# First batch's v sums taken from float32 operands, a weight decode without maximum and mask, eleven-column statistics and a new instruction order, in an attention and gated-MLP kernel on one core

## The chip, the cores and the metric

The kernel runs on one core of a Trainium2 chip. The metric is device time in microseconds (us). Engines are named as the profile names them: PE (matrix products; PEld is its weight load), DVE (vector), ACT (activation), POOL (general) and SP, which here only issues DMAs.

## The reference

Sliding-window attention, whose output is the input of a gated MLP with a spatial gate:

```
scores = q k^T / 8 + slope_h * -|i-j|, masked to 0 <= i-j < 128     # 8 batches, 8 heads, 576 x 64
attn   = softmax(scores);  x = attn v, heads side by side            # x: 8 x 576 x 512
h      = gelu_tanh(x @ w_in);  u, v = halves of h                    # w_in: 512 x 1024
v_n    = (v - mean v) / sqrt(var v + 1e-6) * g_ln                    # along the 512 features
v_s    = w_sg @ v_n + b_sg                                           # along the 576 positions
out    = x + (u * v_s) @ w_out
```

All inputs are float32.

## The kernel before

The kernel works through 32 pairs of heads (four a batch) and, for each batch, through an MLP. Its schedule is one hand-searched list, `ORDER`, in which every step has a short name; the list is the program order on each engine, since each instruction is tied to the one before it on its engine. An instruction that waits therefore holds all that stands behind it on its engine.

Steps of pair n: `q` and `L` load; `a`, `c` are the scores (`*` both at once, from pair 5 on), line 247; `A` `B` `C` `G` add the bias and take minima on DVE (lines 273, 266); `e` `E` `f` `F` `j` exponentials on ACT (line 282); `R` adds 1e-9 to the sums and inverts them on DVE (lines 294, 295); `r` `s` `S` scale on POOL (line 299); `t` `T` `z` transpose on PE (lines 309, 322); `X` `Y` copy the transposes out with masks on DVE (line 318); `2`/`3` and `v`/`V` multiply with the values on PE (lines 329, 342); `x` gathers the result in float32 (`xf`), `h` and `l` split it into a high and a low part in fp32r (`xs`, lines 356, 359).

A product of float32 numbers in the MLP is made of three fp32r products, high x high, high x low and low x high, by `mm3` (lines 559 to 561). Weights arrive as int64 views of float64 and are decoded (`split64`): `i` loads, `d` scales the low word and takes the absolute value of the high word on ACT (lines 179, 181), `m` (line 183) takes a maximum on DVE, `b` (185) shifts and masks, `o` (187) puts the sign and top exponent bits back, `+` (190, POOL) adds the low word, `H` (192, ACT) writes the high part, `-` (194, DVE or POOL by turns) the low part. Twelve tiles are decoded: `w_in` as 0 to 7 (0 to 3 hold the half for v) and `w_out` as 8 to 11. The decoded float32 tile of `w_in` is kept in `scratch` (named `tmp` in the trace), whose memory later becomes `vn`.

Steps of the MLP of batch b: `v` and, in batch 0, `w` sum x times the v half; each of the four row blocks t is the sum of four 128-row pieces c, so batch 0 has 16 such steps, `w{t}{c}` and `v0{t}` for the last c. `tt` sums the last 64 rows. `vg`, `tg` are the gelu (line 633, 658); `n..b/p/c/h` and `vn`/`tn` the normalisation (lines 579 to 595). `u{b}{f}{i}` sums the u half, `uc` copies and `ug` is its gelu; `y{b}{f}{i}` is the spatial product (lines 559 to 561, 706, 707), `gm` `gh` `gl` gate it and split it (lines 712, 716, 719), `O`/`Oa` is the output product, `oa` adds x (line 742), `D` stores (line 754).

So `u000` is the first u product of batch 0 and `y000` its first spatial product. A pool of two PSUM buffers, `ps_m`, serves all MLP sums in the order of their allocation.

Of the kernel before, what the change touches and what calls it, by code (L numbers as in the profile page):

```python
# [21 lines left out]
def attention_gmlp(  # L22
# [148 lines left out]
    def split64(hi, lo, w, f, last):  # L171


        w0 = w.bitcast(U32).rearrange("p (n t) -> p n t", t=2)[:, :, 0]
# [6 lines left out]
        nc.scalar.activation(f, w1f, AF.Abs)
        yield
        nc.vector.tensor_scalar(f, f, TINY64, None, ALU.max)
# [8 lines left out]
        nc.scalar.activation(hi, f, AF.Copy)  # L192
        yield
        last.tensor_tensor(lo, f, hi.bitcast(F32), ALU.subtract)
        yield
# [581 lines left out]
    for b in range(B):  # L777
# [7 lines left out]
        T2 l1 q5 d6 G3 z2 +4 Y2 a4 F3 L3 P2 j3 -2 A4 22 v2 k1 H4 m6 e4 R3 -4 B4 i3 w21 x2 o5 c4 b6 h2 L5 r3 w11 j4 s3 C4
        w31 E4 G4 S3 t3 f4 w01 X3 F4 l2 i10 T3 d3 z3 Y3 +5 w12 q6 P3 k2 R4 *5 o6 H5 m3 i11 -5 b3 w22 A5 s4 q7 w32 +6 e5
        B5 23 w02 v3 j5 o3 i8 C5 S4 E5 H6 G5 +3 L4 x3 f5 r4 t4 -6 h3 T4 X4 d11 l3 i9 z4 Y4 H3 d8 -3 m11 k3 v03 P4 m8 F5
        b11 24 v01 b8 R5 v4 o11 vg03 o8 vg01 s5 nv30b v02 x4 r5 v00 nv30c nv10b nv30p t5 z5 S5 d9 X5 +11 nv30h T5 P5 +8
        d10 Y5 nv10p H11 35 m10 H8 V5 vn03 -11 vg00 nv10c u000 nv00b -8 L6 x5 nv10h b10 *6 vn01 nv00c vg02 L7 o10 u001 A6
        +10 nv20b u010 nv00p uc00 B6 q8 nv20p nv00h nv20c H10 u011 vn00 nv20h bl m9 C6 -10 tt0 uc01 G6 vn02 u020 bH b9  # L790
        tj0 u021 o9 tg0 b- u030 nt0b +9 uc02 nt0c H9 u031 nt0p -9 nt0h *7 uc03 tn0 ug0 y000 q9 A7 B7 h5 y020 h4 l5 C7 G7
        y001 l4 j6 k5 F6 y021 k4 E6 gm00 f6 e6 y010 gm02 E7 R6 s6 j7 y011 gh00 S6 f7 gh02 gl00 y030 gm01 e7 gh01 r6 gl02
        F7 z6 t6 y031 P6 X6 gl01 R7 T6 s7 gm03 Oa0 Y6 gh03 S7 gl03 *8 r7 O02 q10 A8 e8 B8 E8 C8 O00 j8 G8 f8 36 z7 oa00
        t7 V6 P7 oa02 F8 D00 D02 R8 s8 T7 L9 x6 X7 O03 S8 h6 Y7 l6 r8 37 k6 oa03 V7 D03 O01 L8 x7 h7 l7 *9 oa01 k7 D01
# [10 lines left out]
        S14 oa10 v23 Y13 r14 D10 vg22 nv22b t14 vg23 nv22c u230 x12 nv22p nv32b nv22h 313 nv32c V13 vn22 nv32p u231 L15
        x13 X14 nv32h *15 uc23 vn23 ug2 L14 y210 A15 h13 B15 h12 z14 l13 y220 q17 P14 C15 l12 G15 k13 T14 y211 Y14 e15
        E15 *16 gm21 F15 f15 y200 gh21 q19 A16 j15 gl21 B16 e16 y221 E16 C16 R15 f16 G16 y201 s15 gm22 F16 S15 gh22 t15
        gm20 j16 y230 gl22 gh20 R16 k12 gl20 314 y231 r16 s16 V14 gm23 S16 gh23 r15 Oa2 gl23 x14 X15 h14 l14 T15 O23 Y15
        k14 z15 t16 oa23 P15 O20 D23 315 T16 oa20 V15 D20 O21 L16 x15 X16 h15 Y16 l15 L17 *17 oa21 k15 u300 A17 q18 e17
# [5 lines left out]
        z19 y331 gm31 P19 gh31 gl31 V17 gm33 gh33 Oa3 gl33 L18 x17 X19 h17 l17 T19 O32 Y19 k17 z18 t18 oa32 P18 319 O30
        D32 V19 oa30 D30 T18 L20 x19 X18 O33 h19 Y18 l19 k19 318 oa33 V18 D33 O31 L21 x18 h18 l18 *20 oa31 k18 D31 u400
        A20 e20 B20 tt4 j20 C20 f20 G20 u401 tj4 E20 F20 *21 uc40 R20 s20 u430 q22 A21 r20 tg4 S20 B21 t20 q23 v40 C21
        e21 nt4b E21 j21 nt4c u431 f21 G21 nt4p nt4h X20 T20 v41 F21 tn4 uc43 Y20 R21 v42 vg40 r21 s21 vg41 nv04b S21
        nv14b nv04p v43 nv14c nv04c nv14p nv04h nv14h vn40 z20 u420 vn41 vg42 P20 vg43 nv24b *22 nv34b nv24p nv34c u410
# [58 lines left out]
```

## Time and profile before

| | us |
|---|---|
| median of 3 runs | 641.43 |
| lowest, highest run | 639.53, 645.07 |
| the profiled execution's span, first to last instruction | 639.6 |
| PE busy in it | 606.7 |
| DVE, ACT, POOL busy in it | 385.3, 356.2, 236.7 |

In these slices of a fortieth of the span a digit is the busy share in tenths:

```profile
PE   4877789999999999999999999999999999999997
DVE  5899788445854587545753577547664465452611
```

The span is the profiled execution's own time, 1.8 us under the median of the runs. Times in the views count from the span's start. A group's row reads: line, engine, operation, written tile<-read tiles, shapes, xcount | busy us, mean ns of one | idle time before it and what ended it.

### The profile page before, as it was taken

The numbers are of one execution on the slowest core, as the hardware profiler recorded it, in microseconds if no ns is written. First come the engines' busy times: TensorE is split into PE (matmuls) and PEld (weight loads), VectorE is DVE, ScalarE is ACT, GpSimd is POOL, SyncE is SP. The second block draws the span as 40 slices with busy tenths as digits, with TensorE's granted clock in tenths as the row PEclk, the third lists the DMA queues.
The fourth block names the chain that finished last, engine by engine and source line by source line (L and its number), as shares of the span: only waits on it lengthen the run. The fifth ranks groups of instructions, "written<-read, shape, count | busy, mean of one in ns | idle before, by whom it ended". The sixth has DMA issues, their size and how long they took to land.

```text
span 639.6 us, 14817 instructions
## 1 busy us (share of the span) xinstructions
PE 606.7 (95%) x5664; PEld 552.6 (86%) x5664; DVE 385.3 (60%) x1297; ACT 356.2 (56%) x1045; POOL 236.7 (37%) x237
## 2 busy tenths in 40 slices
PE   4877789999999999999999999999999999999997
...
DVE  5899788445854587545753577547664465452611
...
GB/s 277 261 214 180 107 116 38 1 172 57 40 114 70 141 38 104 71 78 98 93 38 58 173 38 76 79 95 115 40 93 73 103 94 40 40 39 38 0 1 75
DMA packets 55931, 57.24 MB, mean 89 GB/s; under 512 B 8498, under 2 KB 45362, under 8 KB 55860
## 3 DMA queue, kind: packets, MB, share of 16 engines
...
## 4 chain that ended last, share of the span: by engine, by line
PE 84%; DVE 8%; ACT 2%; issue 2%; POOL 1%; DMA 1%; SPq 0%; POOLq 0%; DVEq 0%
PE ps_m L559 20%; PE ps_m L561 19%; PE ps_m L560 19%; PE ps_s L342 7%; PE ps_s L247 4%; PE ps_a L309 4%; PE ps_a L247 3%; DVE e L266 2%; DVE px L318 2%; PE ps_a L342 1%; PE ps_m L707 1%; PE ps_m L706 1%; DVE tmp L187 1%; PE ps_m L643 1%; PE ps_m L645 1%
## 5 line engine op out<-in xcount | busy, mean ns | idle before, releaser
L282 ACT ACTIVATE e<-e,stats 128x128 f32<-128x128 f32 (+1 forms) x320 | 121.1, 380 | 33.8 <-DVE stats L266 32.5
L299 POOL TENSOR_TENSOR e<-e,rr 128x512 f32<-128x512 f32 (+1 forms) x96 | 79.9, 853 | 130.4 <-DVE rr L295 103.0
L559 PE MATMUL ps_m<-ws,vn 128*128 128x288 f32 x256 | 79.1, 309 | 0.0
L559 PE MATMUL ps_m<-g,wo 128*128 128x288 f32 x256 | 78.8, 308 | 0.0
L559 PE MATMUL ps_m<-xs,wi 128*128 128x288 f32 x256 | 78.4, 306 | 0.1
L561 PE MATMUL ps_m<-g,wo 128*128 128x288 f32 x256 | 75.9, 296 | 0.0
L561 PE MATMUL ps_m<-xs,wi 128*128 128x288 f32 x256 | 75.7, 296 | 0.0
L561 PE MATMUL ps_m<-ws,vn 128*128 128x288 f32 x256 | 75.7, 296 | 0.0
L560 PE MATMUL ps_m<-xs,wi 128*128 128x288 f32 x256 | 75.6, 295 | 0.0
L560 PE MATMUL ps_m<-ws,vn 128*128 128x288 f32 x256 | 75.6, 295 | 0.0
L560 PE MATMUL ps_m<-g,wo 128*128 128x288 f32 x256 | 75.0, 293 | 0.5 <-POOL g L719 0.5
L359 POOL TENSOR_TENSOR xs<-xf,xs 128x576 fp32r<-128x576 f32 x32 | 45.8, 1432 | 77.8 <-ACT xs L356 77.6
L318 DVE TENSOR_TENSOR px<-ps_a,m_old 128x512 f32<-128x512 f32 x64 | 43.9, 687 | 49.5 <-PE ps_a L309 37.0
L584 POOL TENSOR_TENSOR rs<-rs,mhalf 128x1 f32<-128x1 f32 (+1 forms) x40 | 32.6, 814 | 96.7 <-DVE rs L581 90.1
L719 POOL TENSOR_TENSOR g<-u,g 128x576 fp32r<-128x576 f32 x32 | 45.5, 1423 | 52.3 <-ACT g L716 52.2
L282 ACT ACTIVATION_READ_ACCUMULATOR e<-e,stats 128x1 f32 (+1 forms) x320 | 60.1, 188 | 0.0
L742 DVE TENSOR_TENSOR xf<-ps_m,xf 128x576 f32<-128x576 f32 x32 | 24.1, 757 | 58.4 <-PE ps_m L561 58.4
L712 DVE TENSOR_TENSOR u<-ps_m,u 128x576 f32<-128x576 f32 x32 | 24.2, 755 | 51.2 <-PE ps_m L707 51.2
L559 PE MATMUL ps_m<-wi,xs 128*128 128x512 f32 x128 | 53.7, 419 | 0.5 <-ACT wi L192 0.5
L247 PE MATMUL ps_s<-qk 64*64 64x192 f32 (+2 forms) x632 | 42.5, 351 | 11.3 <-DMA qk<-qkT 7.3
L559 PEld LDWEIGHTS ps_m<-xs,wi 128*128 128x128 f32 x256 | 48.3, 189 | 4.1 <-issue 1.9
L561 PE MATMUL ps_m<-wi,xs 128*128 128x512 f32 x128 | 51.2, 400 | 0.7 <-POOL xs L359 0.7
...
## 6 DMA issues: line engine op xcount, KB each, us to landing
...
outT<-xf SPq DMA_DIRECT2D x32, 288.0 KB, 2.1
...
wst<-w_sgT SPq DMA_DIRECT2D x4, 288.0 KB, 5.9
vd<-v_in SPq DMA_DIRECT2D x64, 16.0 KB, 2.6
```

What stands on the lines that cost most here:

```text
L247: return lambda: nc.tensor.matmul(dst, qk[js, 0, q0:q0 + R], qk[js, 1, k0:k1], start=True, stop=True)
L282: nc.scalar.activation(x, x, AF.Exp, bias=self.nm[0:n, i:i + 1], scale=-1.0, accum_out=self.sm[0:n, i:i + 1])
L299: nc.gpsimd.tensor_tensor(x, x, self.rr[0:n, i:i + m].rearrange("p (m o) -> p m o", o=1).broadcast_to([n, m, c]), ALU.mult)
L309: burst([lambda t=t: nc.tensor.transpose(ct[:, t * P:(t + 1) * P], self.pr[j][:, t, :], ident) for t in range(T)])
L318: nc.vector.tensor_tensor(xv[:, :, :, i, :], cv, m.rearrange("p (t h c) -> p t h c", t=1, h=1).broadcast_to([P, T, 2, R]), ALU.mult)
L342: return lambda: nc.tensor.matmul(x1[heads[j], q0 + lo // 2 * R if t < 0 else q0 + t * R:q0 + (hi + 1) // 2 * R], block, px[j][:, (half * ...
L359: nc.gpsimd.tensor_tensor(lo_of(self.xs), self.xf, hi_of(self.xs).bitcast(F32), ALU.subtract)
L559: nc.tensor.matmul(dst, ah, bh, start=(first and i == 0), stop=False)
L560: nc.tensor.matmul(dst, ah, bl, start=False, stop=False)
L561: nc.tensor.matmul(dst, al, bh, start=False, stop=(last and i == n - 1))
L584: nc.gpsimd.tensor_tensor(x["rs"][0:rows], x["rs"][0:rows], mhalf[0:rows], ALU.pow)
L719: nc.gpsimd.tensor_tensor(st[f"g{f}"][:, 1, :], st["u"][:, f, :], st[f"g{f}"][:, 0, :].bitcast(F32), ALU.subtract)
```

## The change

1. `m` is gone: the absolute value is taken with a scale that makes the rebased exponent come out by a plain shift, `b` shifts without a mask, and `o` takes only the sign from the source. The twelve DVE instructions of line 183 go.
2. In batch 0 each of the 16 steps `w`/`v0` is one float32 product, of `xf` and `scratch`, in place of the three fp32r products of `mm3`. They wait for `x` and `+` in place of `h`, `l`, `H` and `-`.
3. The statistics tiles and `rr` have eleven columns for each half in place of ten; the eleventh holds ones.
4. The normalised `vn` of batch 0 may be written once all eight `-` steps are done (before: 7 and 3), since `scratch` is read by the products now.
5. `ORDER` is another list, without the `m` steps. It differs nearly everywhere.

```diff
-    TINY64 = 2.0 ** -15
+    REBASE = 2.0 ** (-(1023 - 127) // 8)
...
-        x = const.tile([P, 2, NS], F32, name=f"stats{i}")
+        x = const.tile([P, 2, NS + 1], F32, name=f"stats{i}")
...
-        nc.scalar.activation(f, w1f, AF.Abs)
+        nc.scalar.activation(f, w1f, AF.Abs, scale=REBASE)
         yield
-        nc.vector.tensor_scalar(f, f, TINY64, None, ALU.max)
+        nc.vector.tensor_scalar(fi, fi, 3, None, ALU.logical_shift_left)
         yield
-        nc.vector.tensor_scalar(fi, fi, 3, 0x3FFFFFFF, ALU.logical_shift_left, ALU.bitwise_and)
-        yield
-        nc.vector.scalar_tensor_tensor(out=fi, in0=w1, scalar=-0x40000000, in1=fi, op0=ALU.bitwise_and, op1=ALU.bitwise_or)
+        nc.vector.scalar_tensor_tensor(out=fi, in0=w1, scalar=-0x80000000, in1=fi, op0=ALU.bitwise_and, op1=ALU.bitwise_or)
...
-            rr = self.rr = att.tile([P, NS], F32, name="rr", bufs=3)
+            rr = self.rr = att.tile([P, NS + 1], F32, name="rr", bufs=3)
...
-        add(f"m{k}", "DVE", 0.34, at, go, [f"d{k}"], port=True)
-        add(f"b{k}", "DVE", 0.43, at, go, [f"m{k}"], port=True)
+        add(f"b{k}", "DVE", 0.43, at, go, [f"d{k}"], port=True)
...
-        add(k + "h", "ACT", 1.25 if key == "t" else 0.63, at, high, [k + "p", k + "c", f"y{b - 1}{NF - 1}1" if b else "-7", f"y{b - 1}{NF - 1}0" if b else "-3"])
+        add(k + "h", "ACT", 1.25 if key == "t" else 0.63, at, high, [k + "p", k + "c"] + ([f"y{b - 1}{NF - 1}{i}" for i in range(2)] if b else [f"-{c}" for c in range(2 * NC)]))
...
                 for c in cs:
+                    if b == 0:
+                        nc.tensor.matmul(st[key][:, t % 2, :], x[c][:, ts], scratch[:, c, :], start=(c == 0), stop=(c == NC - 1))
+                        continue
...
-                        add(f"w{t}{c}" if c < NC - 1 else f"v{b}{t}", "PE", 0.75, pair_at(c) + OPEN, v_sum(t, [c]), [f"h{c}", f"l{c}", f"-{c}", f"H{c}", f"w{t}{c - 1}" if c else None, f"w{t2}0" if i else None], take=take if c == 0 and i == 0 else [])
+                        add(f"w{t}{c}" if c < NC - 1 else f"v{b}{t}", "PE", 0.75, pair_at(c) + OPEN, v_sum(t, [c]), [f"x{c}", f"+{c}", f"w{t}{c - 1}" if c else None, f"w{t2}0" if i else None], take=take if c == 0 and i == 0 else [])
...
-        i0 q0 i7 d0 wl2 m0 a0 b0 i1 o0 A0 d7 +0 q1 B0 wH2 H0 m7 c0 L1 w-2 d1 C0 -0 G0 e0 b7 wl0 a1 m1 j0 o7 q2 b1 E0 A1
+        q0 a0 wl0 i0 i7 q1 i4 wH0 A0 B0 w-0 d7 d0 d4 b7 b0 o0 +0 E0 e0 j0 c0 C0 G0 f0 F0 b4 o7 R0 L0 a1 A1 B1 i1 d1 i2 e1 s0
...
-        O73 oa72 D72 O71 oa73 D73 oa71 D71
+        O72 oa72 O71 oa71 D63 D62 D72 D70 D60 D73 D61 D71
```

From the first removed line on, the new program's line numbers differ by a few: `R` is on 292 and 293, the new `v` sums on 625, `mm3` on 556 to 558.

DVE in the opening, right after the second block of minima of pair 0 (`C0`, `G0`; rows of line 266 or 264 are its additions and minima). Before:

```order
L273 COPY_PREDICATED ps_s<-sel,ps_s 128x2x64
L266 ISA e,stats_135<-ps_s,bias_108 128x128
L266 ISA stats_135 128x1
L266 ISA e,stats_135<-ps_s,bias_108 128x128
L266 ISA stats_135 128x1
L185 TENSOR_SCALAR tmp<-tmp 128x512
L183 TENSOR_SCALAR tmp<-tmp 128x512
L187 SCALAR_TENSOR_TENSOR tmp<-wst,tmp 128x512
L185 TENSOR_SCALAR tmp<-tmp 128x512
```

Now:

```order
L271 COPY_PREDICATED ps_s<-sel,ps_s 128x2x64
L264 ISA e,stats_135<-ps_s,bias_108 128x128
L264 ISA stats_135 128x1
L264 ISA e,stats_135<-ps_s,bias_108 128x128
L264 ISA stats_135 128x1
L183 TENSOR_SCALAR tmp<-tmp 128x512
L185 SCALAR_TENSOR_TENSOR tmp<-wst,tmp 128x512
L292 TENSOR_SCALAR rr<-stats_135 128x11
L293 RECIPROCAL rr<-rr 128x11
```

Each decode has two DVE instructions now (183 is the shift, 185 the sign) and `R0` follows the decode of tile 4 at once; before, the first blocks of pair 1 stood ahead of `R0`.

PE at the first v sum, after the second part of the scores of pair 2 (line 247, now 245). Before:

```order
L247 MATMUL ps_s<-qk 64x192 x8
L309 MATMUL ps_a<-ident,e 128x128 x8
L559 MATMUL ps_m<-wi,xs 128x512
L560 MATMUL ps_m<-wi,xs 128x512
L561 MATMUL ps_m<-wi,xs 128x512
L322 MATMUL ps_a<-ident,e_1_133 128x128
```

Now:

```order
L245 MATMUL ps_s<-qk 64x192 x8
L307 MATMUL ps_a<-ident,e 128x128 x4
L625 MATMUL ps_m<-tmp,xf 128x512
L307 MATMUL ps_a<-ident,e 128x128 x4
L625 MATMUL ps_m<-tmp,xf 128x512
L320 MATMUL ps_a<-ident,e_1_133 128x128
```

One product stands where three stood, and two row blocks are summed between the transposes of pair 1.

PE just ahead of `u000`, the first product of `xs` with 288 columns. Before:

```order
L309 MATMUL ps_a<-ident,e 128x128 x4
L322 MATMUL ps_a<-ident,e_1_133 128x128
L309 MATMUL ps_a<-ident,e 128x128 x4
L329 MATMUL ps_s<-p_2_130,vd_128 128x64
L342 MATMUL ps_s<-px,vt 64x64 x2
L342 MATMUL ps_s<-px,vt 64x128 x12
L342 MATMUL ps_s<-px,vt 64x64 x4
L559 MATMUL ps_m<-xs,wi 128x288
```

Now:

```order
L340 MATMUL ps_a<-px,vt 64x64 x2
L340 MATMUL ps_a<-px,vt 64x128 x12
L340 MATMUL ps_a<-px,vt 64x64 x4
L625 MATMUL ps_m<-tmp,xf 128x512 x2
L307 MATMUL ps_a<-ident,e 128x128 x4
L556 MATMUL ps_m<-xs,wi 128x288
```

Before, all of pair 5 (`t5 z5 T5 35 V5`) stood ahead of `u000`; now only `t5` does, and `z5`, `T5`, `35`, `V5` come among the u products.

More of the change, by code (lines that the diff above doesn't have):

```diff
@@ L785, in attention_gmlp @@
[L785 to L794, printed above, removed]
@@ L805, in attention_gmlp @@
[L805 to L809, printed above, removed]
@@ L815, in attention_gmlp @@
[L815 to L819, printed above, removed]
@@ L835, in attention_gmlp @@
-        328 t29 vn61 nv06h V28 vn60 tj6 u621 x28 X29 tg6 u630 uc62 nt6b u610 nt6c nt6p u631 nt6h tn6 u611 uc63 T29 uc61
-        y600 Y29 h28 ug6 l28 *31 k28 y620 A31 B31 y601 C31 e31 f31 G31 y621 gm60 F31 gh60 y630 j31 gm62 gl60 E31 gh62 329
-        R31 V29 gl62 s31 y610 L31 x29 r31 S31 h29 z31 t31 l29 P31 y611 X31 L30 k29 y631 gm61 gh61 *30 gl61 gm63 gh63 Oa6
-        gl63 A30 e30 B30 T31 j30 C30 O61 Y31 f30 E30 G30 F30 331 V31 R30 oa61 s30 D61 S30 t30 x31 O60 X30 r30 h31 z30 P30
-        oa60 l31 T30 Y30 D60 O63 k31 330 oa63 V30 D63 O62 x30 h30 l30 oa62 u700 k30 D62 tt7 u701 tj7 uc70 u720 tg7 u721
@@ new lines, in attention_gmlp @@
+        w11 23 B5 R4 v3 C5 -6 e5 E5 j5 f5 G5 -5 x3 w02 tl i11 i10 wl1 L4 gb L5 s4 r4 S4 h3 k0 F5 t4 X4 v03 T4 vg03 l2 l3 -2
+        w12 z4 v01 Y4 P4 H3 24 w22 v4 nv30b -3 R5 nv30c nv30p vg01 wH1 d11 v00 nv30h x4 v02 nv10b s5 vn03 nv10c b11 vg00
+        nv10p k3 k1 nv10h o11 vn01 vg02 +11 t5 u000 u001 u010 nv00b nv20b nv00p uc00 d10 nv00c b10 X5 u020 u011 nv00h tH k2
+        uc01 nv20p S5 T5 u021 o10 nv20c t- +10 r5 tt0 z5 Y5 i8 q7 bl q6 i9 nv20h uc02 H11 vn02 vn00 d8 P5 H10 u030 35 V5 tj0
+        tg0 w-1 -10 -11 nt0b nt0c nt0p d9 bH x5 nt0h u031 *6 b- b9 tn0 b8 o8 o9 A6 B6 uc03 y000 y001 y010 ug0 y011 e6 +9 +8
@@ new lines, in attention_gmlp @@
+        l9 l8 h10 x11 h11 oa11 *12 q14 D11 l11 l10 k9 oa12 A12 B12 C12 G12 v20 u200 *13 v21 j12 k11 f12 F12 k10 E12 e12 R12
+        A13 B13 vg20 vg21 s12 t12 u201 u220 nv12b X12 nv02b nv02c nv12c r12 S12 T12 u221 nv12p z12 Y12 nv02p uc20 E13 uc22
+        P12 e13 nv12h k8 O13 tt2 j13 nv02h vn21 C13 G13 F13 *14 vn20 oa13 Oa1 tj2 v22 O10 f13 R13 A14 B14 s13 S13 r13 tg2
+        E14 v23 nt2b C14 nt2c f14 G14 oa10 nt2p u210 D13 L12 312 t13 nt2h tn2 vg22 vg23 e14 nv22b nv22p q15 V12 u211 z13 D12
+        L13 D10 F14 j14 uc21 P13 nv22c X13 nv32b R14 nv32c r14 s14 nv32p S14 u230 T13 u231 Y13 nv22h x12 nv32h uc23 vn22
@@ new lines, in attention_gmlp @@
+        vn23 313 t14 V13 x13 y200 ug2 X14 *15 A15 B15 y210 y201 C15 G15 gm20 T14 Y14 y211 y220 z14 L14 q17 q16 L15 F15 j15
+        e15 gm21 gh21 h13 P14 gh20 f15 gl20 gl21 E15 R15 y221 *16 gm22 A16 B16 C16 y230 G16 y231 gm23 s15 l13 r15 gh22 gl22
+        S15 314 z15 h12 j16 P15 e16 gh23 V14 t15 E16 x14 X15 gl23 T15 Oa2 O20 F16 f16 Y15 315 V15 R16 r16 s16 t16 S16 T16
+        X16 Y16 oa20 O23 oa23 x15 *17 O22 oa22 h15 h14 l14 l12 l15 L16 q19 A17 B17 C17 G17 e17 k15 E17 j17 F17 f17 v30 v31
+        z16 O21 P16 vg30 vg31 R17 r17 s17 316 k13 S17 t17 V16 u300 nv03b nv03c oa21 nv03p nv13b nv13p z17 D21 L17 q18 X17
@@ new lines, in attention_gmlp @@
+        x18 gl33 h18 k19 O30 *20 l18 A20 oa30 B20 C20 k18 tt4 G20 tj4 O33 f20 E20 F20 *21 A21 oa33 e20 j20 tg4 B21 R20 O32
+        s20 S20 v40 t20 nt4b C21 oa32 X20 nt4c G21 nt4p r20 T20 v41 z20 L20 D33 L21 q22 q23 D30 E21 f21 nt4h tn4 u400 Y20
+        u401 P20 vg40 *22 uc40 vg41 j21 nv04b nv04c nv14b nv14p nv14c nv14h A22 O31 v42 e21 vn41 B22 oa31 nv04p v43 nv04h
+        F21 R21 r21 z21 s21 S21 vn40 C22 G22 e22 f22 E22 P21 vg43 vg42 j22 u430 320 t21 T21 V20 X21 Y21 nv34b x20 nv34c
+        nv24b u420 u431 F22 R22 nv34p s22 nv24p *23 A23 S22 r22 B23 C23 G23 nv24c u421 nv34h uc43 u410 uc42 F23 nv24h E23
@@ new lines, in attention_gmlp @@
+        tg5 R25 nt5b nt5c s25 S24 T24 nt5p uc50 P24 nt5h Y24 tn5 v53 vg53 vg52 t25 L24 q27 D40 D43 L25 q26 D41 nv35b nv35p
+        324 v50 v51 V24 r25 z25 u510 nv25b nv25c nv35c nv25p nv25h nv35h vn53 vn52 vg50 vg51 S25 nv15b nv15c X25 x24 P25
+        u511 *27 nv05b nv05c A27 nv15p nv15h uc51 u520 u530 T25 u521 nv05p nv05h vn50 B27 u531 j27 uc52 vn51 C27 G27 E27 F27
+        uc53 ug5 Y25 *26 A26 B26 C26 G26 f27 f26 F26 E26 y500 y501 gm50 e26 325 O42 oa42 y520 gh50 j26 e27 y521 V25 x25 R26
+        R27 gm52 s26 r27 gl50 y510 t26 y511 X26 y530 z27 gm51 q29 D42 L27 L26 gh52 h25 gh51 P27 S26 l25 T26 s27 gl52 S27 r26
```

70 lines of the change are left out of this document (34 added, 36 removed).

## The prediction

> **What bounds the kernel now.** I read the page first, then the busy times of four stretches cut at two instants that the PE timeline gives, then the groups of the first stretches.
>
> ```profile
> span 639.6 us, 14817 instructions
> PE 606.7 (95%) x5664; PEld 552.6 (86%) x5664; DVE 385.3 (60%) x1297; ACT 356.2 (56%) x1045; POOL 236.7 (37%) x237
> ```
>
> ```profile
> core 0: us, PE busy (x) PEld busy (x) DVE busy (x) ACT busy (x) POOL busy (x), PEclk, DMA share, GB/s
> 0.00:20.00 20.00, 8.87 (x80) 5.69 (x80) 13.28 (x64) 16.55 (x56) 9.19 (x20) 1.00 0.86 280
> 20.00:105.20 85.20, 69.62 (x677) 56.09 (x674) 75.56 (x223) 52.86 (x164) 50.89 (x45) 0.92 0.49 151
> 105.20:635.70 530.50, 528.20 (x4914) 490.85 (x4910) 295.66 (x1009) 286.74 (x828) 176.62 (x173) 1.00 0.24 73
> 635.70:639.60 3.90, 0.00 (x1) 0.00 (x0) 0.76 (x1) 0.00 (x0) 0.00 (x0) 1.00 0.19 76
> ```
>
> The third stretch runs from the first spatial product (`y000`) to the last matmul: PE is busy 528.2 of 530.5 us. Nothing but PE work counts there. The change takes none from it, so what it can win lies ahead of 105.2 us. In the second stretch DVE is the fullest engine, 75.6 of 85.2 us, and PE idles 15.6 us. It splits at `u000`:
>
> ```profile
> 86.77 0.40 PE L559 MATMUL ps_m<-xs,wi 128*128 128x288 f32 x1
> 105.20 0.40 PE L559 MATMUL ps_m<-ws,vn 128*128 128x288 f32 x1
> ```
>
> Between these two rows PE runs almost without a gap; before them it waits. So the question is when `u000` starts, and how much PE work follows.
>
> **An anchor.** Ahead of `Y4` (the masked copy of pair 4) both lists hold the same 57 DVE steps, in different order, but for eight `m` that are gone. Before, `Y4` starts and ends here:
>
> ```profile
> 69.58 0.68 DVE L318 TENSOR_TENSOR px<-ps_a,m_old 128x512 f32<-128x512 f32 x1
> 70.18 0.68 DVE L318 TENSOR_TENSOR px<-ps_a,m_own 128x512 f32<-128x512 f32 x1
> ```
>
> It ends at about 70.8 us. I move this end by what the change does ahead of it.
>
> *The eight maxima.* The groups of DVE up to 105.2 us:
>
> ```profile
> L183 DVE TENSOR_SCALAR tmp<-tmp 128x512 f32<-128x512 f32 x12 | 7.7, 639 | 3.3 <-ACT tmp L181 3.3
> L294 DVE TENSOR_SCALAR rr<-stats 128x10 f32<-128x10 f32 x6 | 3.7, 609 | 0.0
> ```
>
> Eight at the mean of 639 ns are 5.1 us. But part of the mean is a wait. Rows of the timeline show it:
>
> ```profile
> 38.99 1.26 DVE L183 TENSOR_SCALAR tmp<-tmp 128x512 f32<-128x512 f32 x1
> 34.89 0.42 DVE L183 TENSOR_SCALAR tmp<-tmp 128x512 f32<-128x512 f32 x1
> 47.82 1.23 DVE L294 TENSOR_SCALAR rr<-stats 128x10 f32<-128x10 f32 x1
> 47.51 1.52 POOL L194 TENSOR_TENSOR wi<-tmp,wi 128x512 fp32r<-128x512 f32 x1 [2.54 <-ACT wi L192]
> ```
>
> The same operation takes 0.42 or 1.26 us, and a ten-column one took 1.23 us until POOL's instruction was through (47.51 + 1.52 = 49.03; 47.82 + 1.23 = 49.05). Where a maximum waited for POOL, the decode step behind it may wait in its place. Bounds: 8 x 0.42 = 3.4 us (only the work) and 5.1 us; I take 3.7, nearer to the work, since a decode step follows most of them.
>
> *The statistics.* Five of the six `R` stand ahead of `Y4`. After 105.2 us the same instruction is short:
>
> ```profile
> L294 DVE TENSOR_SCALAR rr<-stats x26: 153/172/748, 115.6 to 567.9; 128x10 f32<-128x10 f32 x26
> ```
>
> If eleven columns escape the wait, 5 x (0.609 - 0.172) = 2.2 us go; if not, nothing. No row shows eleven, so I take half, 1.1. [...]
>
> *The v sums.* Three fp32r products follow each other at 0.23 us, 0.70 for a step:
>
> ```profile
> 34.98 0.40 PE L561 MATMUL ps_m<-wi,xs 128*128 128x512 f32 x1
> 35.21 0.40 PE L559 MATMUL ps_m<-wi,xs 128*128 128x512 f32 x1
> 35.44 0.40 PE L560 MATMUL ps_m<-wi,xs 128*128 128x512 f32 x1
> ```
>
> No float32 product of this shape is in the trace. The nearest is the product with the values, 960 columns for each of two heads:
>
> ```profile
> 131.88 1.81 PE ps_s L342 x36
> 75.67 3.40 PE ps_a L342 x36
> ```
>
> If the two heads ran one after the other, a column cost 1.81 / 1920 us and 512 of them 0.48; if side by side, 1.81 / 960 and 0.97. Bounds for a step: 0.48 (a gain of 0.22) and 0.97 (a loss of 0.27). A head's product fills 64 of the 128 output rows, so I take side by side and, without its starts and ends, 0.92: +0.22. Thirteen such steps stand ahead of `Y4`: 2.9 us more PE work. [...] PE idles there, so about half shows: +1.4 (bounds -2.9 and +3.5). PE's waits in the stretch from 20 to 105.2 us, three of them:
>
> ```profile
> PE ps_a L322 <- DVE px L318: 6.5, 3, 3.5
> PE ps_m L561 <- POOL xs L359: 0.7, 1, 0.7
> PE ps_m L559 <- ACT wi L192: 0.5, 1, 0.5
> ```
>
> That a v sum waits for `x` and `+` alone, not for the splits `h`, `l`, `H`, `-`, saves what the last two rows show, 1.2 us off the place where DVE is behind; I price it at nothing. So also the other small edits: the absolute value with a scale and the shift without a mask stay single instructions. And the loads: SP now issues `q0` first, and `A0` can begin about a microsecond sooner than after
>
> ```profile
> 7.30 1.77 PE L247 MATMUL ps_s<-qk 64*64 64x64 f32 x24 [7.30 <-DMA qk<-qkT]
> ```
>
> but the decode of tile 0, which stood ahead of it on DVE (`m0` `b0` `o0`), comes behind it now, and `b4` waits for one more 512 KB load than `b0` and `b7` did; the one is set against the other.
>
> So `Y4` ends at 70.8 - 3.7 - 1.1 + 1.4 = 67.4 us.
>
> **From `Y4` to `u000`.** Before this took 16.0 us: PE ran at half speed (the second row of line 342 above, 3.40 against 1.81 us), waited for a load (first row below), and finished pair 5 first. In the new list only `24`, one sum, `v4`, two sums and `t5` stand between: from
>
> ```profile
> 69.78 3.71 DMA vd<-v_in
> ...
> 73.63 0.66 PE ps_a L329 x2
> ...
> 81.16 0.45 PE ps_a L309 x4
> ```
>
> and the rows above, 0.33 (the 0.66 is at half speed) + 0.92 + 1.81 + 1.84 + 0.45 = 5.4 us at full speed, 10.8 at half. I take 7.0, since the stretch itself is dense. Then a new wait: `u000` takes the PSUM buffer of the first v pair, which `vg00` empties; `vg00` stands on ACT behind `nv30h`, which now waits for the last v sum (its memory is the `scratch` read by it), and needs a `vg` buffer that `vn03` on DVE frees.
>
> ```profile
> L592 ACT ACTIVATE vn<-vg,rs 128x512 fp32r<-128x512 f32 x32 | 22.6, 721 | 24.3 <-POOL rs L584 13.7 <-DVE vg L587 10.5
> L595 DVE SCALAR_TENSOR_TENSOR vn<-vg,rs,vn 128x512 fp32r<-128x512 f32 x32 | 23.5, 746 | 6.6 <-ACT vn L592 6.5
> L633 ACT ACTIVATE vg<-ps_m 128x512 f32<-128x512 f32 x32 | 18.1, 597 | 18.3 <-PE ps_m L561 15.9 <-DVE vn L595 1.8 <-PE ps_a L322 0.3
> ```
>
> 0.72 + 0.75 + 0.60 = 2.1, plus 0.2 for hand-overs, less `t5`'s 0.45: 1.8 us. Queued behind it on PE is all the rest. `u000` starts at 67.4 + 7.0 + 1.8 = 76.2 us, against 86.8.
>
> **From `u000` on.** To `y000` PE took 105.20 - 86.77 = 18.4 us. Now `z5`, `T5`, `35`, `V5` lie in it (0.1 + 0.45 + 0.33 + 1.81 = 2.7) and `*7` has gone behind it, 1.5:
>
> ```profile
> 142.80 0.87 PE ps_a L247 x18
> 143.73 0.65 PE ps_s L247 x14
> ```
>
> That is 19.6 us, so `y000` is at 95.8. From there 530.5 us as before plus `*7`: 627.8. The other engines' work keeps its size, and the new list leaves between a scores step and its transposes at least as much PE work as the old one did (summed with the durations of these rows, 8.7 us at the least, 8.1 before), so I count no new gap.
>
> **The end.** 3.9 us before. Now `D60` and `D61` stand behind `D72` on SP, so that five stores of 288 KB are issued one after the other as soon as `oa72` is through, and `D71` is the sixth.
>
> ```profile
> 628.00:632.00 4.00, 4.00 (x33) 4.00 (x32) 0.76 (x1) 0.00 (x0) 0.00 (x0) 1.00 0.36 140
> ...
> 635.74 0.76 DVE xf L742
> ```
>
> ```profile
> outT<-xf SPq DMA_DIRECT2D x32, 288.0 KB, 2.1
> ```
>
> The first row holds two stores: 0.36 of all DMA engines for 4 us, 0.72 us each. A store alone lands 2.1 us after its issue, 1.4 of it not transfer. `O71` is 24 products of 0.13 us, 3.2 in all, so the five start 3.2 - 0.8 = 2.4 us before the last matmul, and the sixth is through -2.4 + 1.4 + 6 x 0.72 = 3.3 us after it; alone it would be 0.8 + 2.1 = 2.9. That is 0.4 later. Sum: 627.8 + 3.9 + 0.4 = 632.1 us, 7.5 less than the profiled 639.6. That execution is 1.8 us under the median, so I forecast 641.4 - 7.5 = **633.9 us**.
>
> **Rivals.** *PE is the bound of the opening too.* PE idles 15.6 us between 20 and 105.2 us, and the new products add work there. If only half of this idle time can be filled, `y000` is at 105.2 - 7.8 + 3.5 / 2 = 99.2; with 1.5 for `*7` and 0.4 that is 4.1 less, 637.3. For it: 69.6 busy of 85.2. Against: its longest waits were for DVE (line 322 above). *All goes well*: 5.1 and 2.2 at the anchor, 5.4 at full clock, no wait at `u000`: 70.8 - 7.3 + 1.4 + 5.4 + 19.6 = 89.9, 13.4 less than 105.2 with the same additions, so 628.0. *The clock*: PE stays at half speed all through the opening, as it did for the row of 3.40 us. A float32 sum then takes 1.93, 1.2 more than an fp32r step at full speed, and since sums stand between the transposes on which DVE waits, all of it is on the path: 13 x 1.2 = 16.0, `Y4` at 82.0, `u000` at 94.6, `y000` at 114.2: 10.9 more, 652.3. It decides from about 9 us of such losses on. Against: the granted clock was 0.92 in that stretch, and longer products leave fewer gaps. [...]
>
> ```profile
> 44.69 0.30 PE L322 MATMUL ps_a<-ident,e 128*128 128x128 f32 x1 [3.45 <-DVE px L318]
> 44.91 1.63 PE L247 MATMUL ps_s<-qk 64*64 64x64 f32 x24
> ```
>
> **How the numbers follow.** Forecast 0.5, PE-bound 0.27, all well 0.15, clock 0.06, something else 0.02. A measurement here tells about 1% from no change, that is 635.0 and 647.8 us. The forecast lies just under the lower mark, so its half goes about 6 to 4; with all of "all well" and a little of the PE-bound case: faster 0.53, same 0.41, slower 0.06. Range 627 to 641: from just below "all well" to past the PE-bound case with its additions; the clock is left out.
>
> **What would show it.** Right: no DVE row of 512 columns at the old maximum; `Y4` ending near 67 us; the v sums 0.9 us apart; `u000` near 76 and `y000` near 96, with PE busy all but 2 or 3 us from there to the last matmul. Wrong: eleven-column `R` rows of 0.6 us or more beside POOL (the term of 1.1); v sums of 1.9 us (clock); PE without gaps before `u000` and still late (PE-bound); gaps of PE after 100 us, or a last store landing more than 5 us after the last matmul.

## The result and the profile after

| | before | after |
|---|---|---|
| median of 4 runs, us | 640.48 | 648.21 |
| lowest, highest run | 638.23, 645.07 | 645.52, 648.38 |
| the profiled execution's span | 639.6 | 646.4 |
| `Y4` ends | 70.9 | 76.5 (forecast 67.4) |
| `u000` starts | 86.8 | 83.8 (76.2) |
| `y000` starts | 105.2 | 104.4 (95.8) |
| last matmul ends | 635.7 | 642.0 (627.8) |
| behind it | 3.9 | 4.4 (4.3) |

The changed kernel is 1.06% slower (ratio 1.0106, interval 1.0074 to 1.0138), where 1.2% faster was forecast. The same views as before, the page first:

```profile
span 646.4 us, 14780 instructions
PE 607.9 (94%) x5648; PEld 549.5 (85%) x5648; DVE 388.3 (60%) x1285; ACT 363.9 (56%) x1055; POOL 231.1 (36%) x237
```

DVE has 12 instructions fewer (1285 against 1297) and is busy 3 us more. Something on it became longer. The stretches, cut at `u000`, `y000` and the last matmul of this execution:

```profile
0.00:20.00 20.00, 6.96 (x65) 4.77 (x66) 9.39 (x56) 15.00 (x50) 5.96 (x18) 1.00 0.83 265
20.00:83.82 63.82, 49.02 (x447) 32.33 (x446) 56.73 (x165) 40.50 (x144) 36.43 (x34) 0.95 0.48 142
83.82:104.42 20.60, 20.60 (x187) 19.39 (x187) 17.40 (x29) 12.99 (x26) 11.14 (x10) 0.92 0.44 139
104.42:642.00 537.58, 531.28 (x4954) 493.04 (x4950) 304.00 (x1037) 295.42 (x839) 177.57 (x176) 1.00 0.24 72
```

Two things are to be seen. Between 20 us and `u000` PE idles 14.8 of 63.8 us, so nearly as much as it did up to `y000` before. And the last stretch, which the prediction took for 530.5 us with 1.5 for `*7`, is 537.6: PE has 6.3 us of gaps there (2.3 before) and 3.1 us more busy time.

**The opening.** (VectorE is DVE here, and GpSimd is POOL.) DVE's groups by form between 20 and 104 us:

```profile
L192 DVE TENSOR_TENSOR wi<-tmp,wi 128x512 fp32r<-128x512 f32 x4 | 14.1, 3514 | 0.0
L183 DVE TENSOR_SCALAR tmp<-tmp 128x512 int32<-128x512 int32 x8 | 8.4, 1048 | 2.4 <-ACT tmp L181 2.4
```

The first is the low part `-` of the odd tiles of `w_in` (line 194 before, three of them 4.1 us in the same stretch): four take 14.1 us. Two rows make most of it, `-7` and `-5`; one `b` (`b1`) is too long as well. In DVE's timeline:

```profile
20.20 3.61 DVE L183 TENSOR_SCALAR tmp<-tmp 128x512 int32<-128x512 int32 x1
...
39.96 7.07 DVE L192 TENSOR_TENSOR wi<-tmp,wi 128x512 fp32r<-128x512 f32 x1
...
68.52 5.63 DVE L192 TENSOR_TENSOR wi<-tmp,wi 128x512 fp32r<-128x512 f32 x1
```

No waiting time is printed in front of them; the time is inside the row. What GpSimd (POOL) does meanwhile:

```profile
38.65 2.65 POOL L297 TENSOR_TENSOR e<-e,rr 64x128 f32<-64x128 f32 x3 [1.42 <-DVE rr L293]
41.26 1.27 POOL L188 TENSOR_TENSOR tmp<-tmp,wst 128x512 int32<-128x512 int32 x1
42.50 1.39 POOL L357 TENSOR_TENSOR xs<-xf,xs 128x576 fp32r<-128x576 f32 x1
43.85 1.27 POOL L188 TENSOR_TENSOR tmp<-tmp,wst 128x512 int32<-128x512 int32 x1
45.09 1.39 POOL L357 TENSOR_TENSOR xs<-xf,xs 128x576 fp32r<-128x576 f32 x1
...
67.26 2.39 POOL L297 TENSOR_TENSOR e<-e,rr 128x512 f32<-128x512 f32 x3 [0.43 <-DVE rr L293]
69.61 2.76 POOL L357 TENSOR_TENSOR xs<-xf,xs 128x576 fp32r<-128x576 f32 x2
72.34 1.25 POOL L192 TENSOR_TENSOR wi<-tmp,wi 128x512 fp32r<-128x512 f32 x1
```

GpSimd works without a break from 38.65 to 45.09 + 1.39 = 46.48, each row beginning some 0.04 us before the one ahead has ended; `-7` ends at 39.96 + 7.07 = 47.03, that is 0.55 behind it. `-5` ends at 74.15, and GpSimd's second run at 73.59: 0.56. Alone the instruction takes 0.68. So 6.39 and 4.95 us are lost, and all that stands behind on DVE loses them: `B3`, then `X4` and `Y4`. In PE's timeline the first is a hole, and half clock begins inside it (PEclk, the seventh figure behind the stretch, is 0.50 from 46.6 to 53.4 us):

```profile
41.30 0.54 PE L245 MATMUL ps_s<-qk 64*64 64x192 f32 x2
47.98 1.55 PE L245 MATMUL ps_s<-qk 64*64 64x192 f32 x14 [6.15 <-DVE stats L264]
49.46 2.07 PE L625 MATMUL ps_m<-tmp,xf 128*128 128x512 f32 x2
```

```profile
46.60:53.40 6.80, 5.42 (x37) 3.25 (x41) 4.78 (x22) 3.60 (x19) 0.00 (x0) 0.50 0.46 160
```

**The steady state.** PE's waits from `y000` to the end, of after:

```profile
PE ps_m L556 <- ACT vg L633: 4.9, 2, 2.8
PE ps_a L307 <- ACT p L323: 0.6, 1, 0.6
PE ps_m L557 <- POOL g L719: 0.5, 1, 0.5
```

The first row is new; before, the longest in the same stretch was

```profile
PE ps_a L322 <- POOL e L299: 1.4, 1, 1.4
```

The two new waits are for a gelu of the v sums of batches 6 and 7:

```profile
516.01 0.50 PE L556 MATMUL ps_m<-wi,xs 128*128 128x512 f32 x1 [2.10 <-ACT vg L633]
...
605.40 0.40 PE L556 MATMUL ps_m<-xs,wi 128*128 128x288 f32 x1 [2.76 <-ACT vg L633]
```

Behind the second PE runs at half clock for 3.4 us (PEclk 0.50), which costs some 1.7 by an estimate, half of the 3.4:

```profile
606.40:609.80 3.40, 3.40 (x17) 3.40 (x16) 3.10 (x7) 2.02 (x3) 0.95 (x2) 0.50 0.00 0
```

### The profile page after: what moved, and what is told of

It reads as the page before. It is cut to its first block, busy times and chain, and to the rows that moved or that the text cites. A ratio compares the mean times of both kernels' runs of the same rounds, so it can differ in the third digit from the quotient of the medians.

```text
span 646.4 us, 14780 instructions
## 1 busy us (share of the span) xinstructions
PE 607.9 (94%) x5648; PEld 549.5 (85%) x5648; DVE 388.3 (60%) x1285; ACT 363.9 (56%) x1055; POOL 231.1 (36%) x237
## 4 chain that ended last, share of the span: by engine, by line
PE 84%; DVE 8%; ACT 5%; DMA 1%; issue 1%; POOL 0%; POOLq 0%; DVEq 0%; ACTq 0%
PE ps_m L556 20%; PE ps_m L558 19%; PE ps_m L557 19%; PE ps_s L340 7%; PE ps_a L307 4%; PE ps_a L245 4%; PE ps_s L245 3%; DVE wi L192 2%; ACT e L280 2%; DVE e L264 2%; DMA wst<-w_in 1%; DVE px L316 1%; PE ps_m L643 1%; PE ps_m L707 1%; PE ps_m L706 1%; PE ps_m L645 1%
## 5 line engine op out<-in xcount | busy, mean ns | idle before, releaser
L556 PE MATMUL ps_m<-xs,wi 128*128 128x288 f32 x256 | 79.7, 311 | 3.0 <-ACT vg L633 3.0
L558 PE MATMUL ps_m<-xs,wi 128*128 128x288 f32 x256 | 77.0, 301 | 0.0
L557 PE MATMUL ps_m<-xs,wi 128*128 128x288 f32 x256 | 76.9, 300 | 0.0
L581 POOL TENSOR_TENSOR rs<-rs,mhalf 128x1 f32<-128x1 f32 (+1 forms) x40 | 29.9, 749 | 127.8 <-DVE rs L578 123.6
L556 PEld LDWEIGHTS ps_m<-xs,wi 128*128 128x128 f32 x256 | 49.8, 194 | 5.7 <-ACT vg L633 3.7
L340 PE MATMUL ps_s<-px,vt 128*64 128x128 f32 (+1 forms) x972 | 50.7, 258 | 0.2 <-PE ps_a L320 0.2
L556 PEld LDWEIGHTS ps_m<-g,wo 128*128 128x128 f32 x256 | 48.1, 188 | 3.0 <-issue 1.4
L556 PEld LDWEIGHTS ps_m<-ws,vn 128*128 128x128 f32 x256 | 48.3, 188 | 2.5 <-issue 1.7
```

Of the source, the lines that this page charges most:

```text
L340: return lambda: nc.tensor.matmul(x1[heads[j], q0 + lo // 2 * R if t < 0 else q0 + t * R:q0 + (hi + 1) // 2 * R], block, px[j][:, (half * ...
L556: nc.tensor.matmul(dst, ah, bh, start=(first and i == 0), stop=False)
L557: nc.tensor.matmul(dst, ah, bl, start=False, stop=False)
L558: nc.tensor.matmul(dst, al, bh, start=False, stop=(last and i == n - 1))
L581: nc.gpsimd.tensor_tensor(x["rs"][0:rows], x["rs"][0:rows], mhalf[0:rows], ALU.pow)
```

## The experiments

Theory A: the new list lost the time, by the places of `-7` and `-5` in front of GpSimd's runs, and later by the two waits for a gelu. Theory B: the new code lost it, by the float32 sums. Times of all runs, instants from their profiles; the ratio is to runs of the kernel before in the same session. The instants are of one execution each: runs 4, 9 and 10 have the same list up to `y000`, and there they differ by up to 1.6 us.

| kernel | `Y4` ends | `u000` | `y000` | last matmul | span | ratio, interval |
|---|---|---|---|---|---|---|
| before | 70.9 | 86.8 | 105.2 | 635.7 | 639.6 | 1 |
| after | 76.5 | 83.8 | 104.4 | 642.0 | 646.4 | 1.0106, 1.0074 to 1.0138 |
| 1 no maximum, old list | 68.1 | 82.0 | 100.2 | 630.2 | 634.1 | 0.9944, 0.9920 to 0.9969 |
| 2 and eleven columns | 68.3 | 82.9 | 101.3 | 630.5 | 634.4 | 0.9922, 0.9905 to 0.9939 |
| 3 and float32 sums | 69.1 | 84.0 | 102.3 | 631.5 | 635.4 | 0.9927, 0.9902 to 0.9952 |
| 4 after, two lows later | 66.0 | 73.9 | 93.0 | 633.3 | 637.7 | 0.9948, 0.9926 to 0.9969 |
| 5 after, l0 twice | 75.7 | 84.7 | 105.3 | 642.8 | 647.2 | 1.0126, 1.0097 to 1.0154 |
| 6 after, one more in the run | 78.9 | 87.8 | 108.8 | 646.3 | 650.7 | 1.0170, 1.0139 to 1.0202 |
| 7 after, l1 twice | 72.7 | 81.6 | 100.7 | 639.0 | 643.4 | 1.0070, 1.0028 to 1.0111 |
| 8 after, gelus mended | 77.1 | 84.4 | 105.0 | 636.1 | 640.5 | 1.0032, 1.0016 to 1.0048 |
| 9 = 4 and 8 | 67.6 | 75.4 | 94.5 | 625.6 | 630.0 | 0.9833, 0.9811 to 0.9854 |
| 10 and stores early | 66.1 | 74.0 | 93.1 | 624.2 | 628.1 | 0.9826, 0.9807 to 0.9845 |
| 11 and opening mended | 64.2 | 72.1 | 91.8 | 622.9 | 626.8 | 0.9798, 0.9774 to 0.9821 |

**Code or list: runs 1 to 3.** Run 1 is the kernel before with this edit, and the old list less its `m`:

```diff
-        nc.scalar.activation(f, w1f, AF.Abs)
+        nc.scalar.activation(f, w1f, AF.Abs, scale=REBASE)
-        nc.vector.tensor_scalar(f, f, TINY64, None, ALU.max)
-        yield
-        nc.vector.tensor_scalar(fi, fi, 3, 0x3FFFFFFF, ALU.logical_shift_left, ALU.bitwise_and)
+        nc.vector.tensor_scalar(fi, fi, 3, None, ALU.logical_shift_left)
```

> The kernel before with one of the four parts: the decode without maximum and mask, the old list less its twelve m steps. Theory A (the new list lost the time: on VectorE two of its low-part steps, -7 and -5, stand in front of runs of four or five GpSimd instructions and take 7.07 and 5.63 us instead of 0.68): the code's parts are then worth what the opening's rows say, 8 maxima of 0.42 to 0.64 us on the fullest engine, so 0 to 4 us less than before, 636 to 640 us in the profile. Theory B (the code itself costs the time, by the float32 v sums): this part alone is the same, 0 to 4 us less; it is the base of the next two.

Run 2 adds the columns:

```diff
-        x = const.tile([P, 2, NS], F32, name=f"stats{i}")
+        x = const.tile([P, 2, NS + 1], F32, name=f"stats{i}")
-            rr = self.rr = att.tile([P, NS], F32, name="rr", bufs=3)
+            rr = self.rr = att.tile([P, NS + 1], F32, name="rr", bufs=3)
```

> The kernel before with two parts: decode without maximum and mask, and statistics of eleven columns; old list less the m steps, v sums still of three split products. Both theories: within 1.5 us of the run without the eleven columns, since R with eleven columns still took 1.32 and 1.20 us in the changed kernel. If eleven columns escape GpSimd, up to 2 us less.

Run 3 adds the float32 sums, with their dependencies; it is the changed kernel but for the list:

```diff
+                    if b == 0:
+                        nc.tensor.matmul(st[key][:, t % 2, :], x[c][:, ts], scratch[:, c, :], start=(c == 0), stop=(c == NC - 1))
+                        continue
```

> All of the changed code (float32 v sums too) under the old list less its m steps; only the newly searched list is missing. Theory A (the list lost the time): within 2 us of the run with two parts, so 634 to 641 us, well under the changed kernel's 648. Theory B (the float32 sums lost it, each about 1 us of PE instead of 0.7, 2 us at half clock): at least 4 us above the run with two parts, 643 to 649 us.

All three are 0.6 to 0.8% faster than before, and run 3 shares all code with the changed kernel. So theory B falls: with the same code, the list alone makes 1.0106 out of 0.9927. The maximum is the part that pays: `Y4` 2.8 us earlier. The columns add nothing beyond the intervals, and the rows of `R` say why, ten columns in run 1 and eleven in run 2, both with a longest one of nearly a microsecond:

```profile
L292 DVE TENSOR_SCALAR rr<-stats x32: 154/173/972, 18.5 to 562.5; 128x10 f32<-128x10 f32 x32
```

```profile
L292 DVE TENSOR_SCALAR rr<-stats x32: 153/173/978, 18.5 to 562.7; 128x11 f32<-128x11 f32 x32
```

With the float32 sums `Y4` is 0.8 us later (68.3 to 69.1), less than the 1.6 us between executions, and the ratio is where it was.

**The two low parts: run 4.** Only the list of the changed kernel is edited:

```diff
-  ... a3 A3 -7 B3 21 v1 ... G3 e3 E3 P2 f3 F3 Y2 R3 ...
+  ... a3 A3 B3 21 v1 ... G3 e3 E3 P2 f3 F3 Y2 -7 R3 ...
-  ... f5 G5 -5 x3 w02 ... w12 z4 v01 Y4 P4 ...
+  ... f5 G5 x3 w02 ... w12 z4 v01 Y4 -5 P4 ...
```

> The changed kernel with two entries of its list moved: -7 from in front of B3 to behind Y2, and -5 from behind G5 to behind Y4; nothing else. Theory A: both then meet shorter runs of GpSimd, so up to 6.4 + 4.9 us less at Y4 (end near 66 to 69 us instead of 76.5), u000 near 74 to 77 instead of 83.8, and the whole 6 to 10 us less than the changed kernel: 638 to 642 us. Theory B (or a wait for data in those two rows): Y4 and u000 within 2 us of the changed kernel, 646 to 648 us.

The rows at their new places, `Y4`'s end between them:

```profile
45.10 1.78 DVE L192 TENSOR_TENSOR wi<-tmp,wi 128x512 fp32r<-128x512 f32 x1
...
65.35 0.68 DVE L316 TENSOR_TENSOR px<-ps_a,m_own 128x512 f32<-128x512 f32 x1
65.94 1.17 DVE L192 TENSOR_TENSOR wi<-tmp,wi 128x512 fp32r<-128x512 f32 x1
```

7.07 and 5.63 became 1.78 and 1.17, `Y4` ends 10.5 us earlier, `u000` starts 10.0 and `y000` 11.5 us earlier. But the program gains 8.7: from `y000` to the last matmul it now takes 540.3 us, and PE is busy 2.8 us longer there than in the changed kernel:

```profile
92.96:633.30 540.34, 534.05 (x4954) 495.42 (x4950) 303.98 (x1037) 295.46 (x839) 177.39 (x176) 0.99 0.24 72
```

The same two waits for a gelu stand there, with 10.2 us of half clock behind them in place of 3.4.

**What such a row waits for: runs 5, 6 and 7.** Run 5 computes `l0`, the last instruction of the run, twice:

```diff
-            nc.gpsimd.tensor_tensor(lo_of(self.xs), self.xf, hi_of(self.xs).bitcast(F32), ALU.subtract)
+            for _ in range(2 if self.n == 0 else 1):
+                nc.gpsimd.tensor_tensor(lo_of(self.xs), self.xf, hi_of(self.xs).bitcast(F32), ALU.subtract)
```

> The changed kernel with its list as it is, but the low part of x of pair 0 (l0, the last of the five GpSimd instructions in front of which -7 stands) computed twice, 1.39 us of GpSimd work that nothing waits for. Theory A (the row of 7.07 us is a wait for GpSimd's unbroken run to end): the row grows to 8.4 to 8.5 us, and Y4, u000 and y000 come 1 to 1.5 us later. Rival (the row waits for data, or for one particular GpSimd instruction): 7.07 us as before, and nothing later.

```profile
39.39 7.05 DVE L192 TENSOR_TENSOR wi<-tmp,wi 128x512 fp32r<-128x512 f32 x1
```

```profile
44.51 3.20 POOL L358 TENSOR_TENSOR xs<-xf,xs 128x576 fp32r<-128x576 f32 x2
```

The expectation of theory A missed: 7.05, not 8.4. Two instructions of 1.39 took 3.20 us. The second writes what the first wrote and began 0.08 us after the first had ended (by the trace's own times); `-7` ended at 46.44, 0.55 behind the first. By these rows it had got in at that break, which run 7 tests. The time of the whole says nothing here (its interval overlaps that of the changed kernel). Run 6 puts an instruction into the run that waits for nothing:

```diff
+            if self.n == 0:
+                nc.gpsimd.tensor_tensor(gb, self.xf[:, 0:F], self.xf[:, 0:F], ALU.subtract)
             nc.gpsimd.tensor_tensor(lo_of(self.xs), self.xf, hi_of(self.xs).bitcast(F32), ALU.subtract)
```

> The changed kernel with its list as it is, and one more GpSimd instruction of 512 columns, some 1.27 us, in front of l0. It reads x of pair 0 and writes to the tile gb, which is loaded later, so it waits for nothing in the run and nothing on another engine but that load waits for it. In the run with l0 twice the second instruction began 0.08 us after the first had ended, and the row stayed at 7.05 us. Theory A, made sharper (-7 gets in at the first instant between GpSimd's instructions at which the next doesn't follow at once): the row of 7.07 us grows to 8.3 us, and Y4, u000 and y000 come about 1.3 us later. Rival (a fixed set of things that -7 waits for): 7.07 us, nothing later.

```profile
41.45 8.05 DVE L192 TENSOR_TENSOR wi<-tmp,wi 128x512 fp32r<-128x512 f32 x1
```

```profile
46.57 1.03 POOL L358 TENSOR_TENSOR gb<-xf 128x512 f32<-128x512 f32 x1
47.57 1.39 POOL L359 TENSOR_TENSOR xs<-xf,xs 128x576 fp32r<-128x576 f32 x1
```

The row grew by 0.98, the step from one GpSimd row to the next is 1.00. (It was 1.03 us long, not 1.27. `-7` began 1.5 us later than in the changed kernel for reasons ahead of it, so the later instants of this run are not its effect alone.) Run 7 gives GpSimd more work, too, but makes a break in the middle: the edit of run 5 with `self.n == 1`.

> The changed kernel with its list as it is, but l1, the low part of x of pair 1, computed twice. l1 stands in the middle of the GpSimd run in front of which -7 waits, and the second l1 writes what the first wrote, so it can't follow at once (with l0 twice there was a break of 0.08 us between the two). Theory A in its sharper form: -7 gets in at that break, so its row falls from 7.07 to about 4.5 us although GpSimd has 1.4 us more to do, and the minima behind it come about 2.5 us sooner than in the changed kernel, counted from the start of -7. Rivals (-7 waits for the whole of the run, or for a fixed instruction behind l1): 7.1 us or more, up to 8.5.

```profile
39.23 4.47 DVE L192 TENSOR_TENSOR wi<-tmp,wi 128x512 fp32r<-128x512 f32 x1
```

```profile
40.53 1.27 POOL L188 TENSOR_TENSOR tmp<-tmp,wst 128x512 int32<-128x512 int32 x1
41.77 3.21 POOL L358 TENSOR_TENSOR xs<-xf,xs 128x576 fp32r<-128x576 f32 x2
44.94 1.29 POOL L188 TENSOR_TENSOR tmp<-tmp,wst 128x512 int32<-128x512 int32 x1
```

4.47 us, as expected of theory A: `-7` ended at 43.71, 0.55 behind the first `l1`, while the second was running and two more of GpSimd's instructions were still to come. With an instruction more that does nothing of use `Y4` ended 3.8 us earlier than in the changed kernel, 0.7 of them from ahead of `-7`. (In the time of the whole, runs 7 and after overlap.)

**The end of the program: runs 8 to 10.** Run 8 edits the list at the two gelus; run 9 has the edits of 4 and 8.

```diff
-  ... vg62 v63 vg63 ...
+  ... v63 vg62 vg63 ...
-  v70 vg72 nv27b v73 v71 nv27p nv27c vg70 nv27h vn72 nv07b vg73 ... vn70 u730 u731 vg71 nv37p u710 ...
+  v73 vg72 nv27b v70 v71 nv27p vg73 nv27c nv27h vn72 nv37b vg70 ... vn73 u730 u731 vg71 nv07p u710 ...
```

> The changed kernel with only the two late places of its list mended (vg62 behind v63, batch 7's sums in another order); -7 and -5 stay where they are. If the losses of the opening and of the end simply add up: the two waits of 4.9 us and half of the 3.4 us at half clock go, 646.4 - 6.6 = 640 us in the profile, with Y4, u000 and y000 as in the changed kernel. If the one hides the other: less than 4 us.

> The changed kernel with -7 and -5 moved as in the run with two lows later, and the list mended at the two places where PE waits for a gelu late in the program: vg62 behind v63, and in batch 7 the sums in the order v72 v73 v70 v71 with vg73 ahead of v71's end. If the two waits (2.1 and 2.8 us in the run with two lows later) and the half clock behind them (3.4 and 6.8 us, half of which is lost) are only the list's, 2.1 + 2.8 + 5.1 = 10 us go: 628 us in the profile against 637.7. If the new arithmetic or the memory makes them, they come back elsewhere: 635 to 638 us.

In both runs the row of `L633` is gone from PE's waits; what is left of run 8's is

```profile
PE ps_a L307 <- ACT p L323: 0.6, 1, 0.6
PE ps_m L557 <- POOL g L719: 0.5, 1, 0.5
PE ps_s L340 <- PE ps_a L320: 0.2, 1, 0.2
```

Run 8 came to 640.5 (expected 640), with `Y4`, `u000` and `y000` within 0.6 us of the changed kernel. Run 9 came to 630.0 (expected 628), from 637.7. So the two kinds of place are causes of their own and their effects add: 8.7 and 5.9 apart, 16.4 together. The excess of 1.8 fits the half clock: behind the gelus run 4 lost 5.1 us by it in place of 1.7 (half of 10.2 and of 3.4, the same estimate) and run 9 nothing, but run 9 had 3.4 us of half clock in the opening, which run 4 had not, and came to `y000` 1.5 later. With the same code run 9 is also 5.4 us under the old list (run 3, 635.4): the new list lost 16.4 us at these places and won some 5 elsewhere. The first of the two gelu places is a matter of one word: `v63` and `vg62` use one PSUM tile, and written behind `vg62`, `v63` waits for it. In batch 7 the order of the sums fills both `ps_m` buffers half before it completes either, and `vg73`, which empties the first, stands late, so `u730` has to wait. Run 8 changes both at once; which of them counts is not shown.

Run 10 moves `D60` to `D63` behind `oa60` to `oa63`:

> The run with the lows and the gelus mended, and the four stores D60 to D63 each behind its sum in the list instead of among the last eight. The prediction's term for the end: 0.4 us less. The tail behind the last matmul 3.9 us or less instead of 4.4; else the same, 627.5 us. If early stores disturb the last loads or the sums, 0 to 2 us more.

The stretch behind the last matmul fell from 4.4 to 3.9 us as in the kernel before; the ratios of 9 and 10 overlap.

**A version that beats both: run 11.**

```diff
-  ... b7 b0 o0 +0 E0 e0 j0 c0 C0 G0 f0 ...
+  ... E0 e0 j0 c0 C0 G0 b7 b0 o0 +0 f0 ...
-  ... b1 X0 T0 C1 G1 o1 L1 q2 i6 q3 -0 Y0 ...
+  ... X0 T0 C1 G1 L1 q2 i6 q3 -0 Y0 b1 o1 ...
-  ... x2 b5 o5 C4 t3 w30 X3 G4 T3 w31 z3 w32 w-2 +5 w-3 Y3 ...
+  ... x2 C4 t3 w30 X3 G4 T3 w31 z3 w32 w-2 w-3 Y3 b5 o5 +5 ...
```

> The run with early stores, and three decode steps of the opening moved on VectorE to places where they stand in nobody's way: b7 b0 o0 behind G0 (VectorE waited there for a weight load, and a1 on PE for 4.3 us), b1 behind Y0 (3.6 us at GpSimd's run), b5 o5 behind Y3 (2.3 us). Theory A: 2 to 6 us earlier at y000, 622 to 626 us. Against it: the steps themselves are then late for their sums, or the loads of v bound the opening: y000 within 1 us.

It is 2.0% faster than before and 3% faster than the changed kernel (0.9798 / 1.0106). Of the expected 2 to 6 us at `y000` it got 1.3 (93.1 to 91.8), no more than executions of one list differ there: the wait of 4.1 us in front of `a1` on PE fell to 1.4, but `t0`, behind it, now waits 5.6 us for pair 0's scaling in place of 2.7. The intervals of runs 10 and 11 overlap. All four times of run 11 (627.5 to 629.3) lie under the four of run 10 (629.7 to 631.1), so that some 1.5 us are likely, though not shown clear of noise.

## Why the prediction was wrong

In the profile 632.1 us was forecast and 646.4 measured. Of the 14.3 us between them 9.1 had come by `Y4`; -1.5, 1.0, 5.6 and 0.1 came on the four stretches behind it.

- **The bound** was read rightly: PE from `y000` on, the opening ahead of it.
- **The anchor** is the step that failed: "Ahead of `Y4` both lists hold the same 57 DVE steps, in different order, but for eight `m` that are gone", moved by "what the change does ahead of it". It takes the order for neutral. The same 57 steps with all of the new code end at 69.1 us in the old order (run 3) and at 76.5 in the new one, and `Y4` ends at 66.0 when `-7` stands later among them and `-5` behind them (run 4). So 7.4 of the 9.1 us are the order, and 1.7 the sizes of the terms below. The rows for it stood in the prediction: a maximum of 0.42 or 1.26 us and an `R` that ended with GpSimd. I used them for the steps that were removed, and did not ask in front of which GpSimd work the remaining ones now stand, nor how long that work is: `-7` was held past the ends of five GpSimd instructions, up to that of a sixth, and took 6.39 us beyond its own 0.68.
- **The start**: the earlier load and the moved decode of tiles 0 and 7 were "set against" each other. `Y0` ended at 28.3 us instead of 25.9, with `b1`'s 3.61 us ahead of it; with the decode mended (run 11) it is 24.9.
- **The eight maxima**: 3.7 forecast, 2.8 measured at `Y4` (run 1 against before; one execution each). "The decode step behind it may wait in its place" came true: in run 3 one `b` takes 5.22 us.
- **The eleven columns**: 1.1 forecast, nothing measured. The term was half of 5 x (0.609 - 0.172) us, taken without a row of eleven columns; in the runs such rows waited as long as those of ten (0.978 and 0.972 us at the most).
- **The float32 sums**: 0.92 us each forecast; a product takes 0.86 to about 1.0 us at full clock and 1.87 at half, until the next begins. +1.4 at `Y4` forecast, 0.8 measured. The upper of the two bounds was the right one. The sum left out that only twelve steps stood ahead of `Y4` in the old list: 13 x 0.92 - 12 x 0.70 is 3.6 us of PE work, not 2.9.
- **From `Y4` to `u000`**: 8.8 forecast, 7.3 measured; run 4: 7.9. **To `y000`**: 19.6 forecast, 20.6 measured with 3.4 us at half clock in it; run 4, without: 19.1. With the two low parts moved the opening comes near the forecast, 66.0, 73.9 and 93.0 against 67.4, 76.2 and 95.8. That is luck in part: the three terms at `Y4`, 3.4 us together, measured some 1.8 in the old list (70.9 to 69.1), and the new order brought the rest.
- **"So I count no new gap"** failed, too. Of the steady state I compared only the distance between scores and transposes. The two waits are between the MLP's sums and the gelu that empties their PSUM tile. They and the half clock behind them are 4.9 + 1.7 of the 5.6 us over the forecast there; the other waits are 0.9 us less than before.
- **The end** was right: 4.3 forecast, 4.4 measured.
- **Rivals.** The float32 sums were no bound (run 3). The half clock was there, 6.8 us from 46.6 on, but it began 4.8 us into the hole in front of the scores; run 4, without the hole, has none ahead of `y000`. The row of scores of 1.63 us that the prediction shows there lies mostly ahead of the half clock of the kernel before: its granted clock was 1.00 up to 45.97 us, 1.3 us behind the end of the gap of 3.45, and 0.50 from there to 49.39. That "longer products leave fewer gaps" speaks against half clock was an estimate: in the changed kernel the clock fell 1.0 us behind a gap of 2.76 us (605.40) and stayed at 1.00 for 8.7 us behind one of 2.88 (75.49), and no run shows what brings it down. That the new list itself is worse than the old one, for no reason of the edits, was no rival of mine; it should have been, since a list of 1,672 steps was the larger part of the change.

The trace of before had a plainer row of such a wait, which the prediction doesn't use: an `o` of 3.68 us that ended at 53.78, 0.55 us behind an unbroken run of four GpSimd instructions.

```profile
50.10 3.68 DVE L187 SCALAR_TENSOR_TENSOR tmp<-wst,tmp 128x512 int32<-128x512 int32 x1
```

```profile
49.45 2.39 POOL L299 TENSOR_TENSOR e<-e,rr 64x128 f32<-64x128 f32 x3 [0.42 <-DVE rr L295]
51.80 1.43 POOL L359 TENSOR_TENSOR xs<-xf,xs 128x576 fp32r<-128x576 f32 x1
```
